# DMA transposes, two-bank evacuations and a searched order of work items in a fused attention and MLP kernel

## The chip, the cores and the metric

The kernel runs on one core of one Trainium2 chip. The metric is the device time of one call in microseconds (us). A profiled execution also gives a span, from the first to the last instruction, which is about 1.8 us shorter than the time of the same call. All stages and waits are read from spans. A run is called slow when it is more than 1.5% above the fastest of the same kernel on its chip; ratios use the other runs, called fast, while medians and ranges are over all runs.

The engines are PE (matmuls), DVE, ACT and POOL (elementwise work) and SP (here it only issues DMAs). Each engine works through its own instructions in order. A matmul writes into PSUM, which has eight banks; DVE or ACT must copy the result out ("evacuate" it) before the bank is written again. The profile also records the clock that a throttle grants to PE. 1.00 is full speed and 0.50 is half.

## The reference, cut to what matters

The input is 2048 tokens of width 448. Part A is a layernorm, attention with 16 heads of width 28 in which a token sees itself and every second token before it (8 keys), and an output projection. Part B is a layernorm, an MLP whose hidden columns are shifted in time before the second weight, another layernorm, and an MLP of width 1792.

```python
def reference(A_x, A_wqkv, A_wo, B_x, B_w1, B_w2, B_w3, B_w4):
    ...
    x = A_x
    h = x + _A_ref(_layernorm(x, axis=-1), A_wqkv, A_wo)
    h2 = h + _B_ref(_layernorm(h, axis=-1), B_w1, B_w2, B_w3, B_w4)
    return h2
    # _B_ref: h = gelu(layernorm(x) @ w1); shift four column groups by -1, +1, -2, +2;
    #         x1 = x + shifted @ w2;  return x1 + gelu(layernorm(x1) @ w3) @ w4
```

## The kernel before

The Python program first writes down every instruction as an item with its operands, an estimated duration and a tag. A list scheduler then simulates the engines with these estimates and fixes the order of each engine's instructions. Nothing is decided at run time: if an estimate is wrong, the order is still kept, and the engine waits.

The work goes by four token blocks of 512. Work items are named after their phase: `A1` (layernorm and transpose), `QK` and `V` (projections), `att` (scores, exponentials, mask), `av` (attention times V), `rz` (softmax sums to DRAM and back, to be spread over partitions), `WO`, `B1` (layernorm, W1, GELU), `B2` (W2, residual), `W3`, and `B3` (W4 and the result).

A layernorm leaves tokens on partitions, and a matmul wants features there. So each layernorm is followed by 16 transposes on PE and two copies out of PSUM.

```python
    def inv_std(slot, kind, i0, n, s1=1.0, s2=EPS):          # POOL: 1/std from the variance
        pool("tensor_scalar", 60, out=vtmp[:, slot, i0:i0 + n], in0=mv[:, kind, i0:i0 + n, 1], ...)
        S.add("pool", "tensor_tensor", 400 + 160 * n, out=rstd[:, slot, i0:i0 + n], ..., op=ALU.pow)

    def normalize(slot, kind, i, out_ap, in_ap):             # always DVE
        S.add("dve", "tensor_scalar", 390, out=out_ap, in0=in_ap, scalar1=mv[:, kind, i, 0:1],
              scalar2=rstd[:, slot, i:i + 1], op0=ALU.subtract, op1=ALU.mult)

    def transposes(ls, dst):
        for half in range(2):
            T = tile()                                       # one PSUM bank
            for il in range(4):
                for cc in range(2):
                    c = 2 * half + cc
                    S.add("pe", "transpose", 64.0, out=T(...),
                          in_=lntm[:, ls, il, c * KC:(c + 1) * KC], identity=ident[:])
            copy(dst(half), T(...), 1024, 0.52)

    def phase_QK(t):
        ...
        for c in range(4):
            for which in range(2):
                T = tile()                                   # one bank, one evacuation of 512 columns
                for kc in range(4):
                    mm(T(lambda p: p[:, 0, :]), wqk_p[...], hT[:, par, kc, 8:520], kc == 0, kc == 3, 512)
                copy(qT[:, par, c, :] if which == 0 else kT[:, par, c, 8:520], T(lambda p: p[:, 0, :]), 512)
    # ... V, WO, W1, W2, W3 likewise: one bank per evacuation
    # in the scheduler: of the items that could start within `slack` of the earliest, the first in the
    # program goes first
                    if cand is None or st < cand[0] - slack or (st < cand[0] + slack and op.prio < cand[1].prio):
                        cand = (st, op)
```

Of the kernel before, what the change touches and what calls it, by code (L numbers as in the profile page):

```python
# [15 lines left out]
class _Op:  # L16
    __slots__ = ("idx", "eng", "meth", "kw", "dur", "deps", "users", "sem", "val",
                 "t0", "t1", "clock", "is_dma", "chan", "lat", "acc", "odeps", "tag", "opts", "table", "prio", "group")

    def __init__(self, idx, eng, meth, kw, dur):  # L20
        self.idx = idx; self.eng = eng; self.meth = meth; self.kw = kw; self.dur = dur
        self.deps = set(); self.users = 0; self.sem = None; self.val = 0
        self.t0 = None; self.t1 = None; self.clock = None
        self.opts = None; self.table = None; self.prio = idx; self.group = None
        self.is_dma = False; self.chan = None; self.lat = 0.0; self.acc = False; self.odeps = set()
# [15 lines left out]

def _ap_rects(ap):
# [8 lines left out]
    if onchip:  # L51
        pitch, pn = dims[0]
        p_lo = off // pitch
        f0 = off % pitch
        p_hi = p_lo + pn
        fd = dims[1:]
    else:
        p_lo, p_hi, f0, fd = 0, 1, off, dims
# [21 lines left out]
class _Sched:  # L80
    WRITE_KEYS = ("out", "accum_out", "ap")

    def __init__(self):
        self.ops = []
        self.tag = ""
        self.live = {}
        self.chan_count = {}

    def add(self, eng, meth, dur, chan=None, lat=0.0, opts=None, table=None, **kw):
        op = _Op(len(self.ops), eng, meth, kw, float(dur))  # L90
        op.opts = opts; op.table = table
# [42 lines left out]
        ekey = eng if not (op.is_dma or opts) else ("own", op.idx)  # L134
        for (sp, plo, phi, ivs) in reads:
            L = self.live[sp]
            for (lo, hi) in ivs:
                rep = False
                for e in L:
                    if (not e[1]) and e[2] == plo and e[3] == phi and e[4] == lo and e[5] == hi \  # L140
                            and (not e[0].is_dma) and e[0].eng == ekey:
                        e[0] = op; rep = True; break
                if not rep:
                    L.append([op, False, plo, phi, lo, hi])
# [4 lines left out]
        op.deps.discard(op)  # L149
        self.ops.append(op)  # L150
# [3 lines left out]
    TABLE = 1300.0  # L154

    def schedule(self, dma_bw=180.0, slack=100.0):
        n = len(self.ops)
        children = [[] for _ in range(n)]
        npend = [0] * n
        for op in self.ops:  # L160
            g = op.group
            if g is not None and g.ops[0] is op:
                own = set(g.ops)
                for o in g.ops:
                    if o.eng == "pe":
                        op.odeps |= o.deps - own
        for op in self.ops:
            op.odeps -= op.deps
            op.odeps.discard(op)
            npend[op.idx] = len(op.deps) + len(op.odeps)  # L170
# [43 lines left out]
        table = None  # L214
        dma_free = 0.0
        done = 0
        while done < n:
            best = None
            for e in engs:
                cand = None  # L220
                fr = free[e]
                for op in ready[e]:
# [6 lines left out]
                    if e == "act" and op.table is not None and op.table != table:  # L229
                        st += self.TABLE  # L230
                    if cand is None or st < cand[0] - slack or (st < cand[0] + slack and op.prio < cand[1].prio):
# [9 lines left out]
            if e == "act" and op.table is not None:  # L241
                table = op.table
            op.t0 = st
# [13 lines left out]
            if op.is_dma:  # L257
                free[e] = st + op.dur
                ts = max(st + op.dur, dma_free)
                dma_free = ts + op.lat / dma_bw  # L260
                op.t1 = dma_free + 2000.0
# [6 lines left out]
            for ch in children[op.idx]:  # L268
                npend[ch.idx] -= 1
                rdy[ch.idx].append(op)  # L270
# [46 lines left out]

def _fast_path(nc, es, flag, A_x, A_wqkv, A_wo, B_w1, B_w2, B_w3, B_w4, out):
# [28 lines left out]
    hT = sb("hT", [KC, 2, 4, 520], BF16)  # L347
    qT = sb("qT", [128, 2, 4, 512], BF16)
    kT = sb("kT", [128, 2, 4, 520], BF16)
# [7 lines left out]
    lntm = sb("lntm", [128, 3, 4, D], BF16)  # L357
    actT = sb("actT", [KC, 2, 4, 512], BF16)
# [12 lines left out]
    rstd = sb("rstd", [128, 4, NTL], F32)  # L371
    vtmp = sb("vtmp", [128, 4, NTL], F32)
# [4 lines left out]
    ost = sb("ost", [128, 4, D], BF16)  # L377
# [3 lines left out]
    def mm(out_ap, lhsT, rhs, start, stop, n):  # L381
        return S.add("pe", "matmul", max(n, 64) / 2.4 + 8, out=out_ap, lhsT=lhsT, rhs=rhs, start=start, stop=stop)
# [19 lines left out]

    def tile(n=1):
# [14 lines left out]
    for w_ in range(3):  # L418
# [10 lines left out]
    for a_ in range(2):  # L429
        dve("memset", 32, ap=hT[:, a_, :, 0:8], constant=0.0)  # L430
        dve("memset", 32, ap=kT[:, a_, :, 0:8], constant=0.0)
    dve("memset", 256, ap=wqk_p[:, :, :, 28:32], constant=0.0)
    dve("memset", 1024, ap=msk[:], constant=1.0)
    dve("memset", 480, ap=vt[:, :, :, :, 29:32], constant=0.0)
# [7 lines left out]
    def masks():  # L442
# [12 lines left out]
        pool("memset", 8, ap=gT[:, :, :, HALF + 1:HALF + 2], constant=0.0)  # L455
        for j in range(4):
            dma("wo%d" % j, wo_s[32 * j:32 * j + 28, :, :], wov[j], D * D * 2 // 4)
        dma("w1", w1_s[:], B_w1.rearrange("(c k) n -> k c n", k=KC), D * D * 2)
        dma("w2", w2_s[:], B_w2.rearrange("(c k) n -> k c n", k=KC), D * D * 2)
        dma("w3", w3_s[:], B_w3.rearrange("(c k) n -> k c n", k=KC), D * F * 2)  # L460
        dma("w4", w4_s[:], B_w4.rearrange("(f k) n -> k f n", k=128), D * F * 2)
# [9 lines left out]
    def inv_std(slot, kind, i0, n, s1=1.0, s2=EPS):  # L471
# [3 lines left out]
              in1=mhalf[:, 0:n], op=ALU.pow)  # L475

    def normalize(slot, kind, i, out_ap, in_ap):
        S.add("dve", "tensor_scalar", 390, out=out_ap, in0=in_ap, scalar1=mv[:, kind, i, 0:1],
              scalar2=rstd[:, slot, i:i + 1], op0=ALU.subtract, op1=ALU.mult)
# [9 lines left out]
    def transposes(ls, dst):  # L489
        for half in range(2):  # L490
            T = tile()
            for il in range(4):
                for cc in range(2):
                    c = 2 * half + cc
                    S.add("pe", "transpose", 64.0,
                          out=T(lambda p, o=cc * 512 + il * 128: p[0:KC, 0, :].bitcast(BF16)[:, o:o + 128]),
                          in_=lntm[:, ls, il, c * KC:(c + 1) * KC], identity=ident[:])
            copy(dst(half), T(lambda p: p[0:KC, 0, :].bitcast(BF16).rearrange("p (c n) -> p c n", c=2)), 1024, 0.52)

    def phase_A1(t):  # L500
# [9 lines left out]
        for il in range(4):  # L510
            normalize(0, 0, 4 * t + il, lntm[:, ls, il, :], xin[:, 4 * t + il, :])
        if h == 1:
            pool("tensor_copy", 32, out=hT[:, par, :, 0:8], in_=hT[:, par, :, 512:520])
        transposes(ls, lambda half: hT[:, par, 2 * half:2 * half + 2, 8:520])

    def phase_QK(t):
        S.tag = "QK_%d" % t
        h, par = tok(t)
        if h == 1:
            pool("tensor_copy", 32, out=kT[:, par, :, 0:8], in_=kT[:, par, :, 512:520])  # L520
        for c in range(4):
            for which in range(2):
                T = tile()
                for kc in range(4):
                    j0 = 16 * which + 4 * c
                    mm(T(lambda p: p[:, 0, :]), wqk_p[:, kc, j0:j0 + 4, :].rearrange("p j d -> p (j d)"),
                       hT[:, par, kc, 8:520], kc == 0, kc == 3, 512)
                copy(qT[:, par, c, :] if which == 0 else kT[:, par, c, 8:520], T(lambda p: p[:, 0, :]), 512)

    def phase_V(t):  # L530
        S.tag = "V_%d" % t
        h, par = tok(t)
        for blk, (_, _, k0) in enumerate(BLK):
            T = tile()
            for kc in range(4):
                mm(T(lambda p: p[0:KB, 0, 0:D]), hT[:, par, kc, k0:k0 + KB], wqkv_s[:, kc, 2 * D:3 * D],
                   kc == 0, kc == 3, D)
            copy(vt[0:KB, par, blk, :, 0:28], T(lambda p: p[0:KB, 0, 0:D].rearrange("p (j d) -> p j d", d=28)), D)

    def phase_att(t):  # L540
        S.tag = "att_%d" % t
        h, par = tok(t)
        for c in range(4):
            sl = uctr[0] % 3
            uctr[0] += 1
            for jp in range(2):
                T = tile(2)
                for q0, nq, k0 in BLK:
                    for j in (2 * jp, 2 * jp + 1):
                        mm(T(lambda p, a=j % 2, q=q0, n=nq: p[0:KB, a, q:q + n]),  # L550
                           kT[32 * j:32 * j + 28, par, c, k0:k0 + KB],
                           qT[32 * j:32 * j + 28, par, c, q0:q0 + nq], True, True, 48)
# [4 lines left out]
            T = tile()  # L557
            for blk, (q0, nq, _) in enumerate(BLK):
                for j in range(4):
                    mm(T(lambda p, r=32 * j, q=q0, n=nq: p[r:r + 32, 0, q:q + n]), vt[0:KB, par, blk, 4 * c + j, :],  # L560
                       pt[0:KB, sl, j, q0:q0 + nq], True, True, 48)
            copy(osb[:, par, c, :], T(lambda p: p[:, 0, :]), 512)
        for j in range(4):
            dma("zg%d_%d" % (par, j), zp[32 * j:32 * j + 32, par, :],
                osb[32 * j + 28:32 * j + 29, par, :, :].rearrange("p c n -> p (c n)"), 8192)
# [10 lines left out]
    def phase_WO(t):  # L576
        S.tag = "WO_%d" % t
        h, par = tok(t)
        for il in range(4):
            i = 4 * t + il  # L580
            T = tile()
            for c in range(4):
                mm(T(lambda p: p[:, 0, 0:D]), oT[:, par, c, 128 * il:128 * il + 128], wo_s[:, c, :], c == 0, c == 3, D)
            dve("scalar_tensor_tensor", D, psum=True, out=xin[:, i, :], in0=T(lambda p: p[:, 0, 0:D]), scalar=DOWN,
                in1=xin[:, i, :], op0=ALU.mult, op1=ALU.add)

    def phase_B1(t):
# [7 lines left out]
        for il in range(4):  # L595
            normalize(2, 1, 4 * t + il, lntm[:, ls, il, :], xin[:, 4 * t + il, :])
        a = aslot()
        transposes(ls, lambda half: actT[:, a, 2 * half:2 * half + 2, :])
        for g in range(4):
            T = tile()  # L600
            for c in range(4):
                mm(T(lambda p: p[0:KC, 0, :]), w1_s[:, c, g * KC:(g + 1) * KC], actT[:, a, c, :], c == 0, c == 3, 512)
            act(gT[:, g, par, 1 + 512 * h:1 + 512 * h + 512], T(lambda p: p[0:KC, 0, :]), ACT.Gelu_apprx_tanh, 512)
# [12 lines left out]
    def phase_B2(g):  # L616
        S.tag = "B2_%d" % g
        for k, i in enumerate(GROUPS[g]):
            h, par = tok(i // 4)
            T = tile()  # L620
            for c in range(4):
# [547 lines left out]
```

## Time and profile before

| | before |
|---|---|
| time of a call, median of 3 runs | 251.5 us (250.87 to 252.28) |
| span of the profiled run | 250.6 us |
| PE busy, and idle (span minus busy) | 224.6 us (90%), 26.0 us |
| mean granted clock | 0.921 |

PE is the engine to watch. It can lose time in three ways: it does work that could go elsewhere, it is idle, or it is busy at a reduced clock, when the same matmul takes longer.

The page of the profiled run of the kernel before: its busy times and two of its rows over 40 equal slices of the span (each digit is tenths: 9 is 90% or more):

```profile
PE 224.6 (90%) x1681; PEld 112.9 (45%) x1681; DVE 138.2 (55%) x306; ACT 120.7 (48%) x175; POOL 46.2 (18%) x71
...
PE   0799799999979998898995999899998999899992
...
PEclk9999659999965995589998899999999999999998
```

PE's row is nearly full, but the clock's row has three deep dips. A slice is 6.27 us, so they lie at about 25 to 38, 69 to 81 and 94 to 107 us.

The same by stretches of time. Columns are the stretch in us, its length, busy time and instruction count of PE, of PE's weight loads, DVE, ACT and POOL, then the granted clock, the DMA share and GB/s:

```profile
30.00:40.00 10.00, 10.00 (x94) 3.76 (x93) 6.28 (x12) 4.60 (x7) 0.61 (x1) 0.66 0.13 41
70.00:80.00 10.00, 9.33 (x77) 3.83 (x78) 7.71 (x15) 7.01 (x10) 3.21 (x4) 0.54 0.00 0
100.00:110.00 10.00, 9.20 (x65) 3.77 (x64) 7.90 (x16) 4.99 (x7) 0.55 (x1) 0.58 0.03 5
```

PE is 92 to 100% busy in these and yet runs at 0.54 to 0.66 of its speed.

The chain that ended last, in order of time (start, length, what), around the start of dense matmuls:

```profile
7.79 0.84 POOL rstd L1100
...
8.66 0.43 DVE lntm L1100
...
9.13 1.33 PE ps L1100 x10
...
10.49 1.03 ACT hT L1100
...
11.56 12.00 PE ps L1100 x66
```

The pieces are the last layernorm of the first token block (POOL computes 1/std, DVE normalizes), ten PE transposes, their evacuation, and PE's dense work from 11.56 us on. (Two matmuls that need only the first half of the transposes run from 10.38 us, and then PE waits for the second half.)

Two groups of instructions (busy us and mean ns of one, then idle time before them and what ended it), and a stretch of PE's timeline:

```profile
L1100 PE MATMUL ps<-ident,lntm 128*112 128x128 bf16 x192 | 18.8, 250 | 11.2 <-DVE lntm L1100 11.2
...
L1100 ACT ACTIVATE arena<-ps 128x512 bf16<-128x512 f32 (+1 forms) x67 | 40.0, 597 | 28.0 <-PE ps L1100 27.8
```

```profile
112.12 1.06 PE L1100 MATMUL ps<-ident,lntm 128*112 128x128 bf16 x16
...
133.27 0.16 PE L1100 MATMUL ps<-ones,fbit 128*1 128x1 bf16 x1 [1.97 <-DVE fbit L1100]
134.59 1.62 PE L1100 MATMUL ps<-ident,lntm 128*112 128x128 bf16 x12 [1.15 <-DVE lntm L1100]
```

PE does 192 transposes. A record is 250 ns long on average, but they are pipelined: 16 take 1.06 us, 66 ns each. One of them, at 134.59, waited for a layernorm on DVE, as did the small matmul before it.

### The profile page before, as it was taken

To read this page: it belongs to the slowest core of one execution; us is meant where nothing else is said; L and a number is where in the kernel's file an instruction comes from. 1 tells how busy PE (TensorE), PEld (TensorE's weight loads), DVE (VectorE), ACT (ScalarE), POOL (GpSimd) and SP (SyncE) were. 2 spreads that over 40 slices of the span, in tenths; PEclk is the share of its full clock that TensorE was granted. 3 is DMA by queue.
4 is the path that set the end of the run, shared out by engine and by line. 5 is a ranking of instruction groups with operands and counts; after the bars stand their busy time and mean duration, and the time that the engine had idled before them with its cause. 6 is when DMAs were issued, how large, how long until landed. Compare 5 with 4: busy or idle time off the path is not lost.

```text
span 250.6 us, 4082 instructions
## 1 busy us (share of the span) xinstructions
PE 224.6 (90%) x1681; PEld 112.9 (45%) x1681; DVE 138.2 (55%) x306; ACT 120.7 (48%) x175; POOL 46.2 (18%) x71
## 2 busy tenths in 40 slices
PE   0799799999979998898995999899998999899992
PEld 0336345645533556354544533533554345533550
DVE  7596862595785677877999602700385008700220
ACT  2468836896485649645422575166002740156000
POOL 8512200010031003003017200800016000710000
PEclk9999659999965995589998899999999999999998
DMA  6999900070610052007000000000100000000111
GB/s 164 291 222 232 275 12 5 8 171 5 146 29 0 8 131 44 3 7 173 0 1 3 0 0 0 21 18 0 36 15 25 0 16 23 20 18 0 42 39 42
DMA packets 11696, 14.07 MB, mean 56 GB/s; under 512 B 2136, under 2 KB 10712, under 8 KB 11160
## 3 DMA queue, kind: packets, MB, share of 16 engines
q1 hardware_dynamic: 11672, 13.75, 22.7%
q8 instruction: 15, 0.25, 0.4%
q14 instruction: 9, 0.07, 0.1%
HBM read 11.65 MB, written 1.97 MB: 54 GB/s over the span
## 4 chain that ended last, share of the span: by engine, by line
PE 72%; DVE 16%; ACT 5%; POOL 2%; issue 2%; DVEq 0%
PE ps L1100 72%; DVE st L1100 4%; DVE lntm L1100 4%; ACT pt L1100 3%; DVE xb L1100 2%; POOL rstd L1100 2%; DVE mv L1100 1%; DVE oT L1100 1%; ACT hT L1100 1%; ACT actT L1100 1%; DVE pt L1100 1%; ACT arena L1100 0%; POOL vtmp L1100 0%; DVE xin L1100 0%; DVE msk L1100 0%
## 5 line engine op out<-in xcount | busy, mean ns | idle before, releaser
L1100 PE MATMUL ps<-actT,w_s 112*128 112x512 bf16 (+1 forms) x288 | 64.2, 382 | 1.2 <-DVE mv L1100 1.1
L1100 ACT ACTIVATE arena<-ps 128x512 bf16<-128x512 f32 (+1 forms) x67 | 40.0, 597 | 28.0 <-PE ps L1100 27.8
L1100 PE MATMUL ps<-w_s,arena 128*128 128x448 bf16 x224 | 43.9, 353 | 0.0
L1100 PEld LDWEIGHTS ps<-actT,w_s 112*128 112x128 bf16 (+1 forms) x288 | 25.9, 106 | 37.8 <-ACT arena L1100 15.2
L1100 PE MATMUL ps<-hT,arena 112*128 112x512 bf16 x128 | 39.4, 453 | 0.5 <-ACT hT L1100 0.2
L1100 DVE TENSOR_TENSOR ost<-ps,xb 128x448 bf16<-128x448 f32 x16 | 10.0, 622 | 54.2 <-PE ps L1100 54.1
L1100 ACT ACTIVATE pt<-ps 110x1024 bf16<-110x1024 f32 x32 | 30.3, 1030 | 7.8 <-PE ps L1100 7.8
L1100 ACT ACTIVATE actT<-ps 112x1024 bf16<-112x1024 bf16 x10 | 10.0, 1028 | 44.2 <-PE ps L1100 44.2
L1100 POOL TENSOR_SCALAR vtmp<-mv 128x4 f32<-128x4 f32 (+1 forms) x19 | 4.6, 241 | 143.0 <-DVE mv L1100 142.3
L1100 PEld LDWEIGHTS ps<-w_s,arena 128*128 128x128 bf16 x224 | 21.5, 98 | 20.5 <-DVE xb L1100 0.6
L1100 PE MATMUL ps<-ident,lntm 128*112 128x128 bf16 x192 | 18.8, 250 | 11.2 <-DVE lntm L1100 11.2
L1100 PEld LDWEIGHTS ps<-ident,lntm 128*112 128x112 bf16 x192 | 15.9, 152 | 14.5 <-DVE lntm L1100 12.1
L1100 DVE TENSOR_TENSOR pt<-pt,msk 110x1024 bf16<-110x1024 bf16 x32 | 21.0, 684 | 1.7 <-ACT pt L1100 1.7
L1100 DVE BATCH_NORM_STATS2 st<-xin 128x6 f32<-128x448 bf16 x32 | 19.2, 601 | 2.4 <-DMA xin<-in_A_x_dram 1.9
L1100 PEld LDWEIGHTS ps<-hT,arena 112*128 112x128 bf16 x128 | 11.6, 108 | 17.9 <-issue 6.0
L1100 POOL TENSOR_TENSOR rstd<-vtmp,mhalf 128x4 f32<-128x4 f32 (+1 forms) x19 | 18.5, 972 | 1.6
L1100 POOL TENSOR_TENSOR xb<-xb,xin 128x448 bf16<-128x448 bf16 x16 | 16.7, 1072 | 1.5 <-DVE lntm L1100 1.5
L1100 DVE TENSOR_TENSOR xb<-ps,xb 128x448 bf16<-128x448 f32 x16 | 9.6, 600 | 13.4 <-PE ps L1100 13.1
L1100 PE MATMUL ps<-qT,kT 28*110 28x103 bf16 (+1 forms) x320 | 13.2, 229 | 3.8 <-ACT pt L1100 3.5
L1100 PE MATMUL ps<-wo_s,oT 128*128 128x448 bf16 x64 | 16.2, 403 | 0.4 <-DVE oT L1100 0.3
L1100 PE MATMUL ps<-arena,hT 112*110 112x448 bf16 x80 | 15.8, 353 | 0.0
L1100 ACT ACTIVATE gT<-ps 112x512 bf16<-112x512 f32 x16 | 9.6, 600 | 12.3 <-PE ps L1100 12.3
(52 smaller groups left out, 188.5 us busy)
## 6 DMA issues: line engine op xcount, KB each, us to landing
rzb<-rz_scratch SPq DMA_DIRECT2D x16, 256.0 KB, 4.4
w_s<-in_B_w_dram SPq DMA_DIRECT2D x2, 1568.0 KB, 18.0
out_dram<-ost SPq DMA_DIRECT2D x16, 112.0 KB, 1.7
xin<-in_A_x_dram SPq DMA_DIRECT2D x3, 448.0 KB, 8.9
arena<-in_A_wqkv_dram SPq DMA_DIRECT2D x3, 392.0 KB, 6.2
w_s<-in_B_w_dram SPq DMA_DIRECT2D x2, 392.0 KB, 10.5
xin<-in_A_x_dram SPq DMA_DIRECT2D x4, 112.0 KB, 2.2
wo_s<-in_A_wo_dram SPq DMA_DIRECT2D x4, 98.0 KB
```

The source lines that it names most:

```text
L1100: inst = getattr(eng, op.meth)(**op.kw)
```

## The change

Its intent is to take work off PE and to keep PE fed:

1. 11 of the 12 groups of 16 transposes are done by one DMA each, from chunks of 112 columns padded to 128. The very first group stays on PE.
2. Evacuations take two banks at once, so ACT needs one instruction of 1024 columns for two of 512.
3. A normalize may run on ACT too. ACT computes scale times x plus bias, so POOL computes a bias (minus mean times 1/std) in two more instructions.
4. The weights Wo and W1 to W4 are loaded from POOL's queue; of the attention's weights, V's come first.
5. Each work item has a tag and a rank from a list of 138 tags. I call it the searched order: it looks like the result of a search on the schedule model, but the kernel holds the list alone. The scheduler prefers the lower rank.

The diff changes more than these five: the program order of the phases (`B2` of token group 2, for example, now comes ahead of `W3` of group 1), the scheduler's estimates and rules, and one DMA in place of four for each block's softmax sums.

The core of the diff, with cuts marked:

```diff
+_ORDER = """
+W3_0.04 W3_0.10 W3_0.02 W3_2 W3_2.10 W3_2.00 W3_2.04 W3_2.08 W3_3.12 W3_3.02 W3_3.08 W3_3.06 B2_0.0 B2_0.2 W3_3
 ... (7 more lines of tags)
+QK_2.3 av_3.1 QK_0.0 B3_0.2 V_2.0 A1_3 V_2.3
+"""
 ... (in the scheduler)
+        for op in self.ops:
+            op.prio = (self.rank.get(op.tag, 0), op.idx)
 ... (buffers)
-    lntm = sb("lntm", [128, 3, 4, D], BF16)
-    actT = sb("actT", [KC, 2, 4, 512], BF16)
+    lntm = sb("lntm", [128, 3, 4, 4, 128], BF16)
+    actT = sb("actT", [128, 2, 4, 512], BF16)
 ... (inv_std)
+        pool("tensor_scalar", 60, out=nmr[:, slot, i0:i0 + n], in0=mv[:, kind, i0:i0 + n, 0], scalar1=-1.0, scalar2=None,
+             op0=ALU.mult)
+        pool("tensor_tensor", 60, out=nmr[:, slot, i0:i0 + n], in0=nmr[:, slot, i0:i0 + n], in1=rstd[:, slot, i0:i0 + n],
+             op=ALU.mult)
 
     def normalize(slot, kind, i, out_ap, in_ap):
-        S.add("dve", "tensor_scalar", 390, out=out_ap, in0=in_ap, scalar1=mv[:, kind, i, 0:1],
-              scalar2=rstd[:, slot, i:i + 1], op0=ALU.subtract, op1=ALU.mult)
+        ...
+        S.add("flex", "tensor_scalar", 0, out=out_ap, in0=in_ap, scalar1=m_, scalar2=r_, x=n_, opts={
+            "dve": ("tensor_scalar", dict(out=out_ap, in0=in_ap, scalar1=m_, scalar2=r_, op0=ALU.subtract, op1=ALU.mult), 390),
+            "act": ("activation", dict(out=out_ap, in_=in_ap, func=ACT.Identity, scale=r_, bias=n_), 560)})
 ...
+    def transpose_dma(ls, dst):
+        S.add("sp", "dma_start_transpose", 1900.0, chan="tr%d" % ls, lat=80000.0,
+              out=dst.rearrange("p c (i n) -> p (c i) n", n=128), in_=lntm[:, ls, :, :, :].rearrange("p c i n -> p (c i n)"))
 ... (A1)
-        transposes(ls, lambda half: hT[:, par, 2 * half:2 * half + 2, 8:520])
+        if t == 0:
+            transposes(ls, hT[:, par, :, :])
+        else:
+            transpose_dma(ls, hT[:, par, :, :])
 ... (QK; V, av, WO, B1, B2 and W3 alike)
+            T = tile(2)
             for which in range(2):
-                T = tile()
                 for kc in range(4):
 ...
-                copy(qT[:, par, c, :] if which == 0 else kT[:, par, c, 8:520], T(lambda p: p[:, 0, :]), 512)
+            copy(qk[:, par, c, :, 8:520], T(lambda p: p[:, :, :]), 1024)
 ... (B1, W3)
-        transposes(ls, lambda half: actT[:, a, 2 * half:2 * half + 2, :])
+        transpose_dma(ls, actT[:, a, :, :])
 ... (weights from POOL's queue, program order of the phases, pads set to zero)
+    S.rank = {tag: i for i, tag in enumerate(_ORDER.split())}
```

## The prediction

> What bounds it now. The page: PE 224.6 of 250.6 us (90%), DVE 55%, ACT 48%; the chain that ended last is 72% PE, 16% DVE. Losses on top of dense PE work:
> - The first dense matmul is free to run at 11.6 us (chain in order of time); 4.8 us follow the last one.
> - Clock. In the table by 10 us stretches the granted clock was 0.83 and 0.66 at 20-40, 0.54 at 70-80, 0.74 and 0.58 at 90-110, else mostly 1.00: (1 - clock) x time, summed, is about 17 us. The dips follow stretches where PE waits for exponentials of 1.03 us (67-71, 92-96). The Trainium skill, "TensorE: Matmul & The Clock Gate", Part 1, says an idle window halves the clock; the 0.54 agrees.
> - Layernorm waits: about 4 us at 130-135, 0.7 us three times later.
>
> PE work at full clock, from the timeline: 0.216 us per 512-column matmul (56 in 12.1), 0.189 per 448-column one, 0.066 per transpose (16 in 1.06). QK 27.6, V 15.1, scores 14, attention-times-V 6.7, Wo 12.1, W1 13.8, W2 12.1, W3 48.3, W4 42.4, transposes 12.7: about 205 us.
>
> What changes.
> 1. 11 of 12 transpose groups leave PE: -11.7 us, nearly all on the path, plus their copies (0.69 to 1.03 us each) off ACT and DVE, off the path. Each group gains a DMA latency, which no trace here shows. The Trainium skill, "VectorE: DVE Perf Modes", "The three transpose paths", gives 1309 ns for one 128x128 block; no run here shows it. My estimate for 16 blocks in one DMA is 4 to 6 us (rzb copies of 256 KB take 4.4). The order puts about 10 us of other matmuls before most consumers; I expect 1 to 3 us of stalls in all, likeliest at token block 1's V and where the last W1 block feeds W2.
> 2. Two-bank evacuations: ACT 1.03 instead of 2 x 0.597 us. About 10 us less on ACT, 3 on DVE, off the path. Normalizes shared with ACT relieve DVE, which bounds the transition (20.5 of 22.6 us at 112-135).
> 3. Two more POOL instructions of about 0.2 us per layernorm: every normalize waits for them. About +1 us at the start, also since the V weights now load first; hidden elsewhere.
> 4. Weights on POOL's queue: no gain on the path.
> 5. The order mixes scores with QK, V, Wo and fills layernorm waits with W1 and W3. I expect 3-4 us of waits gone and the clock loss down from 17 to about 10 us. DVE, about 80 us of work before attention ends, keeps that stage from shrinking to PE's own time.
>
> Sum: 250.6 - 11.7 (transposes) - 7 (clock) - 5 (waits) + 1 (start) + 2 (DMA stalls) = 230. Range 220 to 239, 8 in 10; I say 229.5. Faster by over 2%: 0.93; within 2%: 0.05; slower: 0.02.
>
> Signs. Right: PE busy about 205-212 us, 16 transposes left; DMA transposes landing within 6 us; mean clock 0.94 or more (before 0.921); W3/W4 stage dense with gaps under 1 us. Step 5 is wrong if clock dips stay as deep, or PE idles behind exponentials at the end of attention, where the new order bunches the last scores.
>
> What would make it wrong: DMA transposes of 8 us or more, or held on SP behind waits for the softmax sums, stalling PE and dropping its clock after each; POOL held up by issuing DMAs; an order brittle against real durations.

## More of the kernel before

Now three large stages, the first 20 us, from there to W3's first matmul at about 141.6 us, and the rest:

```profile
0.00:20.00 20.00, 11.94 (x55) 5.59 (x56) 14.98 (x48) 9.32 (x13) 9.90 (x25) 1.00 0.98 225
20.00:141.60 121.60, 110.58 (x1094) 61.02 (x1092) 89.97 (x198) 73.79 (x103) 20.24 (x29) 0.85 0.27 62
141.60:250.60 109.00, 102.08 (x536) 46.29 (x534) 33.22 (x62) 37.57 (x61) 16.06 (x18) 0.99 0.06 18
```

PE's idle time is the length minus PE's busy time: 8.1, 11.0 and 6.9 us. The clock of the middle stage is 0.85.

## The result, and the profile after

| | before | after |
|---|---|---|
| time, median (lowest to highest) | 251.69 us (250.87 to 252.28), 4 runs | 237.1 us (233.76 to 238.51), 4 runs |
| ratio of fast runs, 95% interval | | 0.935 [0.924, 0.946] |
| profiled run: span, PE busy, PE idle | 250.6, 224.6, 26.0 us | 232.0, 201.1, 30.9 us |
| mean granted clock of that run | 0.921 | 0.973 |

The change is faster by 6.5%. Two of its four runs, 238.51 and 237.57 us, count as slow, so this ratio rests on two fast runs, whose mean is 235.2 us. A ratio, here and below, is the mean time of one kernel's fast runs over that of the other's fast runs of the same rounds, so it is not quite the ratio of the medians quoted beside it. The predicted 229.5 us is 7.6 us under the median of these runs and 5.7 us under the mean of the fast ones, and the 237.1 us lie inside the predicted range. The profiled run of after happens to be the fastest of its four; the other three had a mean clock of 0.961 to 0.965. On another chip six runs gave 234.9 us (run e1). All outputs are right.

The page of the kernel after, the same rows:

```profile
PE 201.1 (87%) x1505; PEld 102.6 (44%) x1505; DVE 121.6 (52%) x244; ACT 117.2 (50%) x131; POOL 66.4 (29%) x123
...
PE   0289999999999749499778999999999999999992
...
PEclk9999999999999967889999999999999999999998
```

The clock's dips are gone but for one, at about 81 to 104 us, and just there PE's row has a hole (a slice is 5.8 us now). The three stages, W3's first matmul now being at 124.86 us:

```profile
0.00:20.00 20.00, 8.87 (x35) 4.27 (x36) 12.85 (x38) 7.69 (x9) 15.29 (x40) 1.00 0.59 161
20.00:124.86 104.86, 90.00 (x966) 48.82 (x965) 77.87 (x141) 73.32 (x85) 30.70 (x52) 0.95 0.52 119
124.86:232.00 107.14, 102.24 (x505) 49.52 (x505) 30.84 (x66) 36.15 (x38) 20.37 (x32) 0.99 0.16 38
```

| stage | length before, after | PE idle before, after | clock before, after |
|---|---|---|---|
| first 20 us | 20, 20 us | 8.1, 11.1 us | 1.00, 1.00 |
| to W3's first matmul | 121.6, 104.9 us | 11.0, 14.9 us | 0.85, 0.95 |
| the rest | 109.0, 107.1 us | 6.9, 4.9 us | 0.99, 0.99 |

The gain of 18.6 us of span is 23.5 us less busy PE, minus 4.9 us more idle PE. Of the 23.5 us, 11.7 are the 176 transposes at 66 ns. The other 11.8 us are the same matmuls done in less time, which I put down to the better clock. Nearly all is won between 20 us and W3. This pair of profiles flatters the clock: in 31 of the 33 other runs of the kernel before whose clock is on record it was 0.932 to 0.934, not 0.921, and the profile after has the highest clock of its four runs.

The start. The chain that ended last, just ahead of PE's dense work:

```profile
9.27 0.57 POOL rstd L1197
9.83 0.21 POOL nmr L1197
...
10.12 0.20 POOL nmr L1197
...
10.34 1.01 DVE lntm L1197
...
11.39 1.33 PE ps L1197 x10
...
13.83 0.61 PE ps L1197
```

The two `nmr` pieces are new, and there is a pair of them for each of the four tiles. Dense work begins at 13.83 us, 2.3 us later than before, and it begins slowly:

```profile
13.83:17.90 4.07, 4.07 (x10) 1.45 (x11) 3.90 (x13) 0.44 (x1) 2.65 (x6) 1.00 0.00 0
```

Ten matmuls take 4.07 us, about 0.41 us each, where 0.22 is usual. By this spacing PE is still at about half clock here, although the view says 1.00; for a start, the spacing of the matmuls is the better witness. The kernel before starts slowly too, though for a shorter time:

```profile
11.56:12.80 1.24, 1.24 (x3) 0.44 (x4) 0.61 (x1) 0.16 (x1) 0.00 (x0) 1.00 1.09 336
```

The end of attention, on PE's timeline (start, length, what, and in brackets the idle time before it and what ended it):

```profile
81.87 0.45 PE L1197 MATMUL ps<-qk 28*110 28x103 bf16 x10 [2.15 <-ACT arena L1197]
83.77 0.70 PE L1197 MATMUL ps<-qk 28*110 28x103 bf16 x10 [1.44 <-ACT pt L1197]
85.59 5.26 PE L1197 MATMUL ps<-wo_s,oT 128*128 128x448 bf16 x16 [1.13 <-ACT pt L1197]
...
94.67 0.66 PE L1197 MATMUL ps<-pt,vt 110*32 110x103 bf16 x40 [2.19 <-ACT arena L1197]
96.84 3.93 PE L1197 MATMUL ps<-actT,w_s 112*112 112x512 bf16 x10 [1.51 <-DMA actT<-lntm]
```

PE waits here for exponentials (`pt`), for an evacuation on ACT (`arena`), and for the DMA transpose of W1's first block (`actT<-lntm`). From 85.59 us sixteen matmuls need 5.26 us, where sixteen of the same kind need 3.19 us at full clock.

The groups that answer to those of before, ACT's normalizes, and the transposes' own view (issue times on SP in ns, then the time from issue to landing):

```profile
L1197 ACT ACTIVATE arena<-ps 128x1024 bf16<-128x1024 f32 (+1 forms) x34 | 34.8, 1023 | 43.5 <-PE ps L1197 43.3
...
L1197 ACT ACTIVATE lntm<-xin,nmr,rstd 128x448 bf16<-128x448 bf16 x16 | 11.5, 755 | 10.3 <-POOL nmr L1197 10.3
```

```profile
L1197 SPq DMA_TRANSPOSE actT<-lntm x8: 1517/1803/4679, 88.5 to 181.4; - x8
...
DMA to landing us min/median/max: 4.2/4.3/8.3
```

A DMA of 16 blocks lands in 4.2 to 4.3 us, and once in 8.3 us. That one was issued at 88.47 us, right behind four copies of 256 KB each. Of the three transposes ahead of QK and V, which this view leaves out, two took 4.2 and 4.3 us and the first 6.2 us.

### The profile page after: what moved, and what is told of

Its sections match the earlier page's. It is cut to its first block, busy times and chain, and to the rows that moved or that the text cites. A ratio compares the mean times of both kernels' runs of the same rounds, so it can differ in the third digit from the quotient of the medians.

```text
span 232.0 us, 3657 instructions
## 1 busy us (share of the span) xinstructions
PE 201.1 (87%) x1505; PEld 102.6 (44%) x1505; DVE 121.6 (52%) x244; ACT 117.2 (50%) x131; POOL 66.4 (29%) x123
## 4 chain that ended last, share of the span: by engine, by line
PE 64%; DVE 14%; ACT 7%; DMA 6%; POOL 5%; issue 2%
PE ps L1197 64%; DVE st L1197 5%; DMA actT<-lntm 4%; ACT pt L1197 3%; POOL rstd L1197 3%; DMA hT<-lntm 3%; DVE xin L1197 3%; POOL nmr L1197 2%; DVE mv L1197 1%; ACT arena L1197 1%; DVE xb L1197 1%; DVE pt L1197 1%; POOL vtmp L1197 1%; ACT qk L1197 1%; DVE lntm L1197 1%
## 5 line engine op out<-in xcount | busy, mean ns | idle before, releaser
L1197 ACT ACTIVATE arena<-ps 128x1024 bf16<-128x1024 f32 (+1 forms) x34 | 34.8, 1023 | 43.5 <-PE ps L1197 43.3
L1197 DVE TENSOR_TENSOR xb<-ps,xb 128x448 bf16<-128x448 f32 (+1 forms) x24 | 18.3, 771 | 65.5 <-PE ps L1197 65.5
L1197 PEld LDWEIGHTS ps<-actT,w_s 112*128 112x128 bf16 (+1 forms) x288 | 30.4, 107 | 35.5 <-DMA actT<-lntm 4.3
L1197 PE MATMUL ps<-hT,arena 112*128 112x512 bf16 x128 | 32.0, 400 | 1.5 <-ACT hT L1197 1.1
L1197 POOL TENSOR_TENSOR xb<-xb,xin 128x448 bf16<-128x448 bf16 x16 | 16.7, 1073 | 2.4 <-DVE lntm L1197 1.5
L1197 ACT ACTIVATE lntm<-xin,nmr,rstd 128x448 bf16<-128x448 bf16 x16 | 11.5, 755 | 10.3 <-POOL nmr L1197 10.3
L1197 PE MATMUL ps<-qk 28*110 28x103 bf16 (+1 forms) x320 | 12.1, 220 | 4.8 <-ACT arena L1197 2.6
L1197 ACT ACTIVATE qk<-ps 128x1024 bf16<-128x1024 f32 x10 | 10.2, 1024 | 10.7 <-PE ps L1197 10.7
L1197 PE MATMUL ps<-arena,hT 112*110 112x448 bf16 x64 | 14.9, 358 | 0.4 <-DMA hT<-lntm 0.4
L1197 PE MATMUL ps<-w_s,gT 112*128 112x448 bf16 x64 | 12.8, 353 | 1.4 <-ACT gT L1197 1.4
L1197 PEld LDWEIGHTS ps<-qk 28*110 28x110 bf16 x320 | 9.2, 127 | 10.0 <-ACT arena L1197 3.3
L1197 ACT ACTIVATE gT<-ps 112x1024 bf16<-112x1024 f32 x8 | 8.2, 1024 | 9.0 <-PE ps L1197 9.0
```

What stands on the lines that cost most here:

```text
L1197: inst = getattr(eng, op.meth)(**op.kw)
```

## The experiments

Each run below is timed against the kernel before on the same chip. Runs e1 to e4, e5 to e8 and e9 to e12 shared a chip and the runs of the kernel before, whose medians there were 251.0, 251.0 and 250.9 us.

My theory after the result was: the transposes are worth their 11.7 us, the order gives the clock, and the shortfall lies at the start and at the end of attention. The rivals were that the spread of runs explains the shortfall, that the parts do not add up but work only together, and that the losses that I could see are not on the path.

### e1: the kernel after again

No edit, five rounds on another chip.

> The changed kernel as it is, run again to see its spread. Theory A (its runs differ because the clock of the TensorE drops for a window or not at the gaps around the end of attention): times spread over about 4 us, from 234 to 238.5, and the mean granted clock falls as the time rises, as in the first four runs (0.973 at 233.8 us, 0.961 at 238.5). Rival (the spread is of the chip or of the launch): the clock stays within 0.002 while the time spreads. Ratio to before about 0.94.

Measured: 234.91 us (234.49 to 235.73, 6 runs), ratio 0.9375 [0.9341, 0.9409], clocks from 0.958 to 0.969. Neither theory holds: the times spread by 1.2 us, not 4, and the clock by 0.011, and the time does not follow the clock in these six runs. In later runs of near copies on other chips it does: in e10, two runs at a clock of 0.974 or 0.975 took 235.7 us, and four at 0.959 or 0.960 took 238.1 to 238.8 us. So one and the same program can differ by 2 to 3 us, and what puts an execution into the better clock was not tested. I compare the following runs with this ratio of 0.9375.

### e2: all transposes on PE again, searched order kept

```diff
-            transpose_dma(ls, hT[:, par, :, :])
+            transposes(ls, hT[:, par, :, :])
 ...
-        transpose_dma(ls, actT[:, a, :, :])
+        transposes(ls, actT[:, a, :, :])
```

> The changed kernel with all 12 transpose groups back on the TensorE; order list, two-bank tiles and normalizes kept. Theory A (the change gains what leaves the TensorE): 9 to 12 us slower than the changed kernel, about 247 us, TensorE busy about 11 us more. Rival B (the DMA transposes pay for it with their latency, which is 6% or 15 us of the chain that ended last): within 3 us of the changed kernel.

Measured: 258.3 us (257.42 to 259.15), ratio 1.031 [1.026, 1.036]. This is 23 us more than e1, twice what the transposes themselves take, and slower than the kernel before. Neither theory foresaw that. In the profiled runs PE is busy 14.8 us more than in e1 (217.4 against 202.6) and idle 8.0 us more (38.7 against 30.7). PE's waits by total time (us in total, times, longest):

```profile
PE ps L1197 <- ACT lntm L1197: 13.3, 7, 6.8
PE ps L1197 <- ACT actT L1197: 5.2, 4, 2.6
```

PE stands behind normalizes on ACT (13.3 us; 6.8 of them are the first wait at the start, which every kernel has, and the kernel after has 8.8 in all) and behind the evacuations of the transposes (5.2 us). With PE transposes a late layernorm stops PE itself; with DMA ones PE does other items meanwhile. But the scheduler also placed all items anew, so this run mixes the two causes; e9 was made to part them.

### e3: DMA transposes kept, no searched order

```diff
-    S.rank = {tag: i for i, tag in enumerate(_ORDER.split())}
-    S.rank["flag"] = -1
+    S.rank = {}
```

> The changed kernel without its searched order: work items ranked in program order by the same scheduler. If the order is worth what I predicted for waits and clock (about 10 us): 245 to 249 us. Rival (the gain is all from the transposes and the order is worth little): 236 to 240 us.

Measured: 247.84 us (245.15 to 252.9), ratio 0.985 [0.979, 0.991], which at a threshold of 2% counts as unclear. Everything in the change but the searched order is worth about 1.5%, and the searched order a further 12 to 13 us. The fast runs have clocks of 0.931 to 0.944, against 0.958 to 0.969 in e1, so part of what the order gives is clock.

### e4: the kernel before with DMA transposes for W1 and W3

The eight groups ahead of W1 and W3 go by DMA, in 112-column chunks padded to 128 as in the change. The rest of the kernel before, the program order included, is kept.

```diff
-        transposes(ls, lambda half: actT[:, a, 2 * half:2 * half + 2, :])
+        transpose_dma(ls, actT[:, a, :, :])
```

> The kernel before with one thing changed: the 8 transpose groups in front of W1 and W3 go by DMA, in the program order of before. Theory A: 8 x 1.06 us leave the TensorE, about 243 us (0.966). Rival B (without the new order the DMA latency of about 4.3 us each stands in the open): 248 us or more, with waits of the TensorE for the transposed tile of 1 us or more at several of the 8 places.

Measured: 258.03 us (257.2 to 259.4), ratio 1.031 [1.026, 1.036]. PE's work got shorter and the kernel got slower by 7 us. The page's busy line and PE's waits:

```profile
PE 217.7 (85%) x1553; PEld 104.2 (41%) x1553; DVE 135.5 (53%) x301; ACT 109.7 (43%) x164; POOL 49.7 (19%) x73
```

```profile
PE ps L1106 <- DMA actT<-lntm: 15.5, 5, 6.8
```

PE is busy 6.9 us less than before, but it waits 15.5 us for the transposes in five places, up to 6.8 us in one. The clock is lower too: 0.898 to 0.910 in these runs, against 0.932 to 0.934 in the fast runs of before. So in the program order of before these DMA transposes are a loss: their latency lands on the path where no other work stands. The program order of after is another one, and there they are a gain (e9).

### e9: all transposes on PE, no searched order

The edits of e2 and e3 together.

> The kernel after with every transpose on PE again and the list of work items empty (items in program order). It completes the square of transposes (DMA or PE) by order (searched or program): DMA with search 234.9, PE with search 258.3, DMA without 247.8 us. Theory 1 (the two parts are additive; the 258.3 is the price of the PE transposes): about 248 + 23 = 271 us. Theory 2 (the order was searched for the DMA transposes and is a bad one for others; PE transposes cost their own 11.7 us at most): 248 + 5 to 12 = 253 to 260 us, so the searched order is worth nothing, or less than nothing, to the kernel with PE transposes.

Measured: four runs: fast 255.19 and 256.07 us, slow 260.54 and 261.46 us; three rounds were too few for an interval. Set beside the means of the fast runs of e1 to e3, which are from another chip:

| mean of fast runs | searched order | program order |
|---|---|---|
| DMA transposes | 235.1 us (e1) | 246.9 us (e3) |
| PE transposes | 258.3 us (e2) | 255.6 us (e9) |

Theory 2 holds. In program order, PE transposes cost about 9 us, near the 11.7 us that they keep PE busy. With PE transposes the searched order is worth nothing: it is 2.7 us worse by these means, but with two fast runs, and two others at 260.5 and 261.5 us, that is not clear of the noise. With DMA transposes it is worth 12 us. The two parts are worth 20 us together, and apart 9 us and nothing. The table also shows what is easy to overlook: the rest of the change, without these two parts (e9), is no gain over the kernel before but about 5 us slower, by its two fast runs. What a search made for PE transposes would find was not tried, so it is not shown that only DMA transposes allow a good order.

### e5: the start without POOL's two extra instructions

In e5 to e8, e11 and e12 the order is frozen, which means that the scheduler runs as in the kernel after, and only then are single instructions changed in its finished order. In the diffs, angle brackets stand for longer expressions. All other instructions keep their places; I compared the orders engine by engine, and PE's was identical in e5 to e8.

```diff
+    gone = {op for op in S.gorder if op.tag == "A1_0" and op.eng == "pool" and <it writes nmr>}
+    for op in S.gorder:
+        op.deps -= gone
+        if op.tag == "A1_0" and <it is a normalize on ACT>:
+            op.eng = "dve"; op.meth, op.kw, op.dur = op.opts["dve"]
+    S.gorder = [op for op in S.gorder if op not in gone]
```

> The kernel after with every engine's order frozen; only the first layernorm group (4 tiles) is changed: its two extra POOL instructions per tile are taken out, and its normalizes are all the DVE's subtract-and-multiply. Theory (the start is about 4 us longer than before because of the POOL chain ahead of every normalize): first dense matmul about 1.5 to 2 us earlier than 13.83 us, total 2 to 4 us less than the kernel after, ratio to the kernel before 0.922 to 0.930 (the kernel after had 0.9375 in five rounds). Rival (the lost time at the start is made good by waits later, DVE being short of time in attention): within 1 us of the kernel after, ratio 0.934 to 0.942.

Measured: 233.89 us (231.22 to 236.53), ratio 0.9289 [0.9243, 0.9335]. The chain ahead of the dense work:

```profile
8.19 1.13 DVE arena L1211
9.31 0.49 DVE lntm L1211
...
12.27 7.94 PE ps L1211 x28
```

Dense work begins at 12.27 us, 1.6 us earlier than in the profile of after and 1.4 us earlier than in that of e1 (13.67), as expected. By the ratio the whole kernel gains 0.9%, about 2 us; by the medians, which are from two chips, 1.0 us. Part of this is given back: in the profiled runs W3's first matmul comes at 125.07 us, against 125.48 in e1. The theory holds, at the low end of its size or a little under it. The edit removes the two POOL instructions and also moves this group's normalizes from ACT to DVE; the two were not parted. A new piece suggests that the next limit is a copy of weights on DVE (1.13 us at 8.19) that sits ahead of the last normalize.

### e6: layernorm normalizes of W1 and W2 back on DVE

```diff
+    for op in S.gorder:
+        if op.tag[:2] in ("B1", "B2") and <it is a normalize on ACT>:
+            op.eng = "dve"; op.meth, op.kw, op.dur = op.opts["dve"]
```

> The kernel after with frozen orders; only the layernorm normalizes of the W1 and W2 work items that ACT took are given back to DVE at the same place of the order. Theory (at the end of attention ACT works in order, and its normalizes wait for POOL between exponentials that PE needs): 3 to 5 us less, ratio to before 0.918 to 0.927, the waits of PE for ACT's exponentials and for the transpose at 79 to 97 us mostly gone, granted clock there above 0.83. Rival (DVE is what limits attention, so the normalizes are no better there): no gain or 1 to 3 us slower, ratio 0.938 to 0.95.

Measured: 237.12 us (236.39 to 240.29), ratio 0.9444 [0.941, 0.9477], about 1.7 us slower than e1. My theory fell. PE's timeline and waits:

```profile
80.99 0.46 PE L1206 MATMUL ps<-qk 28*110 28x103 bf16 x10 [1.25 <-ACT arena L1206]
81.91 0.46 PE L1206 MATMUL ps<-qk 28*110 28x103 bf16 x10 [0.46 <-ACT pt L1206]
84.18 1.67 PE L1206 MATMUL ps<-wo_s,oT 128*128 128x448 bf16 x3 [1.82 <-DVE oT L1206]
```

```profile
PE ps L1206 <- DVE oT L1206: 4.7, 3, 2.2
```

The waits for ACT did shrink, from 2.15 and 1.44 to 1.25 and 0.46 us. But DVE took the normalizes in order ahead of the products that Wo needs (`oT`), and PE waits for those now: 4.7 us in three places, where the kernel after has 1.7 us in one. The wait moved from one engine to the other.

### e7: e5 and e6 together

> Both of the edits of the two runs before. If they are independent the gains add: 5 to 8 us less than the kernel after, ratio to before 0.906 to 0.918. If a wait on DVE is what limits the stage, the two together give no more than the better of them alone.

Measured: 235.49 us (235.21 to 236.63), ratio 0.9388 [0.9353, 0.9423]. The gains that I expected did not add up, since one of them does not exist; the two measured effects do. From e6 to e7, on one chip, the start's edit is worth 0.6%, which is 1.6 us by the medians.

### e8: every two-bank evacuation cut in two

Each fp32 evacuation of two banks is issued as two instructions of one bank at the same place, except the exponentials, which took two banks in the kernel before as well.

```diff
-            inst = getattr(eng, op.meth)(**op.kw)
+            parts = _halves(op) if prefix == "f_" else [op.kw]     # _halves: one per PSUM bank
+            for kw in parts:
+                inst = getattr(eng, op.meth)(**kw)
```

> The kernel after with frozen orders; every evacuation of two fp32 PSUM banks is issued as two instructions of one bank each, at the same place (ACT 2 x about 0.6 us in place of 1.03, DVE alike). Theory of the prediction (evacuations are off the path): within 3 us of the kernel after, ratio to before 0.935 to 0.95; ACT's busy time up about 8 to 10 us. Rival (the two-bank evacuations carry a good part of the gain): 5 us or more slower, ratio above 0.957.

Measured: 236.22 us (234.15 to 237.2), ratio 0.9404 [0.936, 0.9449]. The interval overlaps that of e1, so no gain from the two-bank evacuations is shown; the ends of the intervals allow at most 2.7 us. That agrees with the prediction, which had them off the path. My figure for ACT was wrong: its busy time grew by 3.3 us (117.2 to 120.5), not 8 to 10, for the profile of this run has

```profile
L1212 ACT ACTIVATE arena<-ps 128x512 bf16<-128x512 f32 (+1 forms) x68 | 36.8, 594 | 41.8 <-PE ps L1212 41.8
```

68 of them at 594 ns each would be 40.4 us one after another, but the group is busy for 36.8 us, so two in a row must overlap.

### e10: weights issued from SP's queue

```diff
-        return S.add("pool", "dma_start", 800.0, chan=chan, ...)
+        return S.add("sp", "dma_start", 500.0, chan=chan, ...)
```

> The kernel after with the weights' loads issued on SP's queue in place of POOL's (the scheduler places the items anew). The prediction said no gain on the path: within 1% of the kernel after, ratio to before 0.93 to 0.95. Rival (POOL's issues delay its layernorm chain, or SP's in-order queue delays the transposes): over 1% off either way.

Measured: 238.07 us (235.69 to 238.82), ratio 0.9491 [0.9444, 0.9537]. This is 1.2% over e1, just outside the 1% that I allowed though inside the ratio that I wrote beside it (0.93 to 0.95), and the intervals do not meet. The order was not frozen here, and the scheduler placed the items anew, so it stays open whether the queue itself or the new order costs these 3 us. The Trainium skill, "DMA: Bandwidth & Descriptors", "Issuing engines are not separate DMA queues", says that another issuing engine saves only the issuing engine's own time. This run does not contradict that, and it does not test it alone.

### e11: e5, and the first W1 layernorm and its transpose earlier

```diff
+    norm = <the four normalizes of B1_0 into lntm>       # all on DVE now
+    tr   = <the DMA transpose of B1_0>
+    at = S.gorder.index(<POOL's 1/std for them>) + 1
+    S.gorder[at:at] = norm + tr                           # taken out of their old places
```

> The frozen start of e5 (ratio 0.929), and in it the four normalizes of W1's first token block moved to DVE right behind their POOL result (about 79 us in place of 80 to 88), with their transpose issued at about 82 us, ahead of the copies of the softmax sums, not at 88 behind them. Theory (the late normalizes and the 8 us landing cost the end of attention its waits): transpose lands in 4 to 5 us, PE's wait for it (1.2 to 2.4 us) gone, 1 to 3 us less than e5, ratio 0.917 to 0.925. Rival (the stage is bound by exponentials and evacuations on the path to the last attention items; the transpose is only the last to arrive): within 1 us of e5.

Measured: 233.36 us (232.2 to 233.81), ratio 0.929 [0.9253, 0.9328], the same as e5. The transposes, and PE:

```profile
DMA to landing us min/median/max: 4.2/4.3/4.3
```

```profile
92.89 0.66 PE L1227 MATMUL ps<-pt,vt 110*32 110x103 bf16 x40 [2.19 <-ACT arena L1227]
94.73 4.49 PE L1227 MATMUL ps<-actT,w_s 112*112 112x512 bf16 x10 [1.17 <-issue]
```

The mechanism was there: issued at 79.39 us, ahead of the copies, none of the eight transposes for W1 and W3 needs more than 4.3 us, and the 8.3 us landing is gone. The gain was not. PE reaches W1 at 94.73 us, only 1.05 us earlier than e5, for it stops behind an evacuation first: the 2.19 us for `arena` are still there, and the 1.17 us after them end with the next evacuation of the same banks. The rival holds: the transpose was only the last of several things to arrive.

### e12: e11, and another PSUM bank for the last attention-times-values tile

```diff
+    for op in <the instructions of av_3.1>:               # banks 0 and 1 in place of 6 and 7
+        <shift its PSUM operand by 6 banks>
+    first("av_3.1").deps |= evac("WO_1.0");  first("WO_2.0").deps |= evac("av_3.1")
```

> e11, and the last attention-times-values tile put into another PSUM bank pair than the tile before it, so that PE does not wait for ACT's evacuation of that one (2.2 us at 93 to 95 us in the kernel after). Theory (the schedule model saw that bank as free in time, because its ACT runs ahead of the real one): that wait falls below 0.5 us, 1 to 2 us less than e11. Rival: the wait moves to the evacuation behind it, no change. Together with e11 it should be the fastest kernel, ratio 0.91 to 0.92.

Measured: 232.6 us (231.07 to 234.16), ratio 0.9274 [0.9226, 0.9323]. PE's timeline at the same place:

```profile
91.57 0.42 PE L1241 MATMUL ps<-pt,vt 110*32 110x103 bf16 x20 [0.39 <-DVE xin L1241]
...
93.19 0.41 PE L1241 MATMUL ps<-pt,vt 110*32 110x103 bf16 x18 [0.69 <-DVE pt L1241]
94.77 4.02 PE L1241 MATMUL ps<-actT,w_s 112*112 112x512 bf16 x10 [1.17 <-issue]
```

The wait of 2.19 us has become waits of 0.39, 0.29 and 0.69 us, yet W1 begins at 94.77 us as in e11. My edit left W1's first tile in its old banks and still waiting for that last evacuation, so the rest of the gain stayed locked in: the wait moved, as the rival said. The difference to e11 is within the intervals. e12 is the fastest kernel, 1.1% under e1 with intervals that do not meet, and it beats both kernels; but e5 alone accounts for most of that, and e5, e11 and e12 cannot be told apart.

## Why the prediction was right or wrong, point by point

**The total.** Predicted 229.5 us (220 to 239), measured 237.1 us, and 234.9 us on another chip. Direction and range were right. In the profiled pair the sum looks near (a span of 232.0 us against about 230), because two errors nearly cancel: the clock gave more than predicted and the waits took more. That is luck, since this pair happened to have a low clock before and a high one after. With the clocks of e1 the clock's gain is near its prediction, and the error of the waits is left standing as the shortfall of about 5 us.

**PE's transposes (minus 11.7 us).** The work left PE as counted: 1681 matmul records became 1505, and PE is busy 201.1 us, below the predicted 205 to 212. But the prediction took this term as standing by itself, "nearly all on the path". It does not: DMA transposes without the new order made the kernel before 7 us slower (e4), and in the new kernel they are worth 9 us in program order and 23 us in the searched order. So the term needs an order that covers the latency. The program order of after does so in part, and the searched order adds to it; which of the differences between e4 and e3 makes the transposes a gain was not tested.

**The clock (minus 7 us).** Right in direction and, for the usual runs, near in size. The sum of (1 - clock) times the span went from 19.8 us (0.921) to 6.3 us (0.973) in the profiled runs, by 13.5 us; with the clocks of run e1 (0.933 before, 0.965 after) it went from 16.7 to 8.2 us, by 8.5 us. The searched order brings a part of it (e3); what sets off a dip was not tested. The prediction puts the dips down to an idle window; the 0.54 fits a halved clock, but ahead of the dip at 69 to 81 us no single wait of PE was over 0.46 us, so one long wait was not what came before it. The Trainium skill, "TensorE: Matmul & The Clock Gate", Part 1, gives 426.7 ns for the start-to-start time of 512-column matmuls at half clock. The trace comes near it: 0.41 us each over the first ten matmuls of the kernel after.

**The waits (minus 5 us), with the start (plus 1 us) and the DMA stalls (plus 2 us): the step that failed.** "I expect 3-4 us of waits gone" became minus 5 in the sum and stood beside two additions, so PE's idle time should have gone from 26.0 to about 24 us. It rose to 30.9 us (30.7 in e1). So the step that failed is step 5's claim that the new order removes waits: it moved and added them. By stage:

- The start was put at plus 1 us. PE's idle time there rose by 3.1 us. Dense work starts 2.3 us later, because POOL's two extra instructions stand ahead of every one of four normalizes, and because the normalizes are split between DVE and ACT: without both (e5) it starts 1.6 us earlier again, and the kernel is 1 to 2 us faster (e5, e7). The other 0.7 us of the delay was not tested.
- The middle stage was to lose 3 to 4 us of waits and gained 3.8 us. The old waits at 130 to 135 us are gone, but new ones stand at the end of attention (79 to 97 us) and behind W1 and W2. The prediction named this as what would prove step 5 wrong: "PE idles behind exponentials at the end of attention". That happened there, with waits of 1.1 to 2.2 us and a clock of 0.66 at 80 to 90 us, while the other dips vanished. By these traces step 5 was right for the first 79 us and wrong for the next 20.
- The DMA stalls were sized nearly right: 2.8 and 0.4 us, predicted 1 to 3 in all. Nine of the eleven transposes landed within the 6 us of the prediction's signs; 6.2 us and 8.3 us were over. The place was half right. V of token block 1 waits 0.36 us, as named; the large ones are W1's first block (1.51 us) and W3's first (0.94 us).

Why the end of attention has these waits is shown only in part. ACT's order is one cause that I argued and that e6 refuted as a remedy: taking ACT's normalizes away moves the wait to DVE. Removing the late transpose gained nothing that can be measured (e11). A bank that is reused too soon holds 2.19 us there, and freeing it moved the wait behind (e12). Several chains end within 1 to 2 us of one another, so removing one of them shows the next. No experiment removed them all, so what this stage could give stays open.

**The evacuations: off the path.** Not contradicted (e8: a gain of at most 2.7 us, perhaps none). But "about 10 us less on ACT" was wrong, since ACT also took 33 normalizes, which it did not have before: ACT went from 120.7 to 117.2 us, and DVE from 138.2 to 121.6 us. A normalize costs ACT 755 ns, and the schedule model assumes 560. I had the means to see this: the Trainium skill, "ScalarE: Activation LUTs", "What ACT_TABLE_LOAD costs", gives 186 ns plus 0.833 ns per element, and about 93 ns more for each pointer operand, which with 448 elements and two pointer operands makes an estimate of 745 ns. The trace agrees with the page, and not with the model: the 33 normalizes on ACT cost it about 6.4 us more than the model saw.

**Weights on POOL: no gain.** Open: moving them back costs 1.2% (e10), with the order changed as well.

**Two small errors of bookkeeping.** I added up a span and gave it as the time of a call. The calls are 1.8 us longer (233.76 and 232.0 us for the same run). And the profile is one execution: this one was 3 us faster than the median of its four.

## What to carry to other kernels

An instruction taken off the busiest engine gives its time only if what replaces it is covered by other work; so cost a DMA in place of a short PE operation together with the order that must hide it. Add up busy time and idle time of the bottleneck engine separately, each before and after, because a total can be near the truth with both terms wrong. Where several chains end almost together, expect that moving one instruction from a full engine to another moves the wait with it.

## What the Trainium skill lacked or had wrong

- "VectorE: DVE Perf Modes", "The three transpose paths", has 1309 ns for one 128x128 block by DMA and nothing for many blocks in one DMA. Here 16 blocks in one DMA landed in 4.2 to 4.3 us, 0.27 us a block, so one block's figure times 16 would be five times too long. Right behind four copies of 256 KB it took 8.3 us, and the first one of the kernel took 6.2 us.
- "DMA: Bandwidth & Descriptors", "Latency and other measured facts", has 261 GB/s for a DMA transpose and no time for a small one. Sixteen blocks of 128x128 in two-byte elements are 0.52 MB; 4.3 us makes that 122 GB/s from issue to landing. Nor does the page say how long a transpose of this size from SBUF to SBUF holds the issuing engine. Here it was 1.3 to 2.0 us for eight of the eleven, 2.9 and 3.5 us for two in the first 52 us, and 4.7 us for the one issued behind the copies.
- "TensorE: Matmul & The Clock Gate", Part 4, gives about 275 ns for a transpose within a kernel. A record is 250 ns long here, which is near, but 16 in a row take 1.06 us. What PE loses is 66 ns a transpose, and that part gives no figure for transposes in a row.
- "GPSIMD Engine Reference", "Elementwise — side-by-side cycle accounting", measures an add of 2048 columns and gives no cost for an instruction of one or four columns. In the kernel after, a power of 128x4 took 1.1 us and one of 128x1 0.57 us on average, and each of the two multiplies that make the bias 0.22 to 0.32 us on average. These stand in front of every normalize.
